# Three more tiles of attention probabilities transposed and split on TensorE, and a smaller slack in the planner

## The chip, the cores and the metric

The kernel runs on one core of one Trainium2 chip. The metric is the device time of one execution in microseconds (us), the median of several runs. Engines carry the names of the profile: PE is TensorE (PEld its weight loads), DVE is VectorE, ACT is ScalarE, POOL is GpSimd, SP is SyncE, which here issues every DMA.

## The reference

Attention within clusters, whose output feeds a feed-forward layer. Queries and keys are each assigned to one of 16 clusters of their head, and a query sees only the keys of its own cluster.

```python
# q, k, v: (4, 8, 768, 64) float32; centroids: (8, 16, 64)
q_assign = argmax(einsum('bhsd,hcd->bhsc', q_n, c_n))      # normalised; the same for k
mask = q_assign[:, :, :, None] == k_assign[:, :, None, :]
scores = where(mask, scale * (q @ k.T), -1e9)
attn = exp(scores - max(scores)); attn = attn / (sum(attn) + 1e-9)
x = (attn @ v).transpose(0, 2, 1, 3).reshape(3072, 512)
h = x @ w_in                                               # (512, 2048)
g = where(h >= 1, h, where(h <= -1, 0, (h + 1) ** 2 / 4))
out = g @ w_out                                            # (2048, 512)
```

## The kernel before

**Units and tiles.** The work is cut into 4 batches, 3 chunks of 256 query rows in each, and 4 pairs of heads: 48 attention units. A unit has 4 score tiles of 128 queries by 768 keys: the two heads `j` of the pair times the two query tiles `t` of the chunk, numbered `n = 2 j + t`. When the 4 head pairs of a chunk are through, their output `x` goes through the feed forward in 8 blocks `f` of 256 hidden columns.

**One score tile.** TensorE makes the scores in a PSUM buffer `pair`, a group of 4 matmuls (`at_scores`); the mask comes in through the second pair of these. VectorE takes them out to `sS` with the row minimum of the negated scores in `sbi`. ScalarE makes the exponential in place and its row sums. The probabilities are then needed transposed and as two halves in float16, a high part and the rest, since the products run in float16 with three terms. There are two ways to that, in `at_soft`:

- By DMA: ScalarE casts `sS` to the high half of `hl`, GpSimd subtracts to the low half, and one transposing DMA brings both to `pT`.
- By TensorE, where `by_tensor` says so: six float32 transposes of `sS` against the identity `idf` go back into the tile's own `pair` buffer, ScalarE casts them to the high half of `pT`, two matmuls with the negated identity `idm` take that half off in place, and a second cast makes the low half. The buffer is held until then.

`at_av` multiplies `pT` with the values into `banka`; ScalarE copies the row factors to `rb`, VectorE multiplies, ScalarE casts the high half of `x`, GpSimd subtracts the low half. `ffn1` makes a hidden block from `x` in one of three banks (`bankh`, `banki`, `bankj`; 24 matmuls), takes it through `r` on VectorE and ScalarE and to `g` in two halves (ScalarE, GpSimd); `ffn2` gathers the products with `w_out` in the second `pair` buffer. So the scores have both `pair` buffers in the prologue (`early()`: steps below 22), and the first one, `pair0`, alone afterwards. The weights are loaded, scaled and split beside all that (`word`, `w`, `wk`, `w_am`, `w_iw`, `w_sw`).

**What sets the order.** Nothing is issued as it is written. Each operation is recorded (all of them at line 322) with a priority, its step. A list planner in the kernel then deals the operations out to the engines: it runs a model with prices, up to 60 rounds of forward and backward passes, and keeps the order that comes out shortest in a replay with noise. `SLACK` is added in the forward pass to the end of every operation that is not a DMA. The order is built into the program; each engine goes through its own in sequence, and waits by semaphores. The first chunk's scores have steps 0 to 15; the second chunk's first head pair has 16 to 19, its second 20 to 23, and a tile's softmax comes one step after its scores.

The lines that the change touches are 39 (`SLACK`) and 960 (the condition of `by_tensor`).

Of the kernel before, what the change touches and what calls it, by code (L numbers as in the profile page):

```python
# [35 lines left out]
PHASES = (0.0, 850.0, 1700.0, 2550.0)  # L36


LATER, LATER_DMA, SLACK = 25, 600, 30


TURN, TURN_WAIT = dict(vector=185, gpsimd=118), 200
# [402 lines left out]
def tile_clustered_attention_moe(  # L445
# [83 lines left out]
    def early():  # L529

        return rec.step < EARLY
# [390 lines left out]
    def at_soft(b, hp, c, j, t):  # L922
# [12 lines left out]
        if by_tensor(b, hp, c, j, t):  # L935
            with rec.group():
                for i in range(T):
                    to = pS[:, i // 3, i % 3 * P : (i % 3 + 1) * P]
                    rec.tensor.matmul(
                        to, sf[:, i * P : (i + 1) * P], idf, start=(i % 3 == 0), stop=False, is_transpose=True,  # L940
                        skip_group_check=True,
                    )
            pt = pS[:, :, :HS].rearrange("p h (n q) -> p h n q", q=P)
            hi, lo = (pT[:, x * T : (x + 1) * T, t, :].rearrange("p (h n) q -> p h n q", h=2) for x in range(2))
            rec.scalar.copy(hi, pt)
            with rec.group():
                for h in range(2):
                    rec.tensor.matmul(pS[:, h, :HS], idm, hi[:, h], start=False, stop=True, skip_group_check=True)
            rec.scalar.copy(lo, pt)
            at_sums(e, n)  # L950
            return
# [5 lines left out]

    def by_tensor(b, hp, c, j, t):

        return early() and b == c == 0  # L960

    def at_sums(e, n):
        if n == 3:
# [317 lines left out]
```

## Time and profile before

| | |
|---|---|
| median of 3 runs | 879.8 us (878.59 to 880.06) |
| the profiled execution, its own time | 879.45 us |
| its span, first to last instruction | 877.7 us |
| TensorE busy | 93% of the span, 7532 matmuls |
| VectorE, ScalarE, GpSimd busy | 75%, 74%, 62% |
| tiles transposed by DMA, by TensorE | 176, 16 |

How to read it: the profile shows one execution. A stretch's busy time tells which engine paces it; what an engine waited for is told by the instruction whose semaphore came last. Matmuls overlap, so the time that a group takes is best read from its start to the start of what follows it. The granted clock is that of TensorE, 1.0 at 2.4 GHz and 0.5 at 1.2 GHz.

### The profile page before, as it was taken

The page shows a single profiled execution, that of the slowest core. Times are in us where ns is not written, and L with a number is a line of the kernel's source. Part 1 is how long each engine was busy: PE and PEld are TensorE (multiplying, and loading weights), DVE is VectorE, ACT ScalarE, POOL GpSimd, SP SyncE. Part 2 cuts the span into 40 slices and gives each one's busy share as a digit, 9 for nine tenths or more (in the row PEclk, how much of TensorE's full clock was granted, in tenths as well). Part 3 has the DMA queues.
Part 4 walks back from the last instruction along what each step waited for, and adds up shares of the span by engine and source line. Part 5 has one row for each costly group of instructions (what it writes and reads, how often), then busy time and mean ns, then how long its engine had stood idle before and what let it go on. Part 6 is the DMA issues. An engine that isn't in the chain of part 4 may idle for free.

```text
span 877.7 us, 19909 instructions
## 1 busy us (share of the span) xinstructions
PE 815.6 (93%) x7532; PEld 565.8 (64%) x7532; DVE 658.1 (75%) x1571; ACT 649.7 (74%) x1150; POOL 540.8 (62%) x534
## 2 busy tenths in 40 slices
PE   3666879899999999999999999999999999999998
PEld 3444556566666766766766666666766667766664
DVE  7999989999779776668787688668887767454232
ACT  6899998788776687777777597788777787676232
POOL 1155497878656778656666676666666667666222
PEclk9999889999999999999999999999999999999999
DMA  9975689779999979899898879999999888676100
GB/s 321 254 198 133 198 176 181 138 148 197 163 182 176 165 142 192 172 174 191 173 204 161 149 129 182 167 173 176 180 182 179 147 150 157 109 133 109 20 25 25
DMA packets 404193, 141.01 MB, mean 161 GB/s; under 512 B 372736, under 2 KB 396288, under 8 KB 404096
## 3 DMA queue, kind: packets, MB, share of 16 engines
q1 hardware_dynamic: 404096, 139.73, 81.2%
q8 instruction: 59, 0.97, 0.4%
q14 instruction: 38, 0.31, 0.1%
HBM read 40.40 MB, written 6.29 MB: 53 GB/s over the span
## 4 chain that ended last, share of the span: by engine, by line
PE 64%; DVE 19%; ACT 6%; DMA 4%; issue 3%; POOL 2%; SPq 0%; ACTq 0%; DVEq 0%; POOLq 0%
PE pair L322 32%; PE banka L322 9%; PE bankh L322 9%; PE bankj L322 7%; PE banki L322 7%; DVE sS L322 5%; DMA pT<-hl 3%; DVE r L322 2%; DVE qn L322 2%; ACT sS L322 2%; POOL hl L322 2%; DVE w L322 1%; DVE banki L322 1%; DVE bankh L322 1%; DVE bankj L322 1%
## 5 line engine op out<-in xcount | busy, mean ns | idle before, releaser
L322 POOL TENSOR_TENSOR hl<-sS,hl 128x768 f16<-128x768 f32 x176 | 295.8, 1687 | 109.8 <-ACT hl L322 83.0
L322 PE MATMUL pair<-w,g 128*128 128x512 f16 x1152 | 270.2, 379 | 0.3 <-ACT o L322 0.3
L322 PEld LDWEIGHTS <-w 128*128 128x128 f16 x2304 | 224.3, 98 | 48.2 <-issue 5.1
L322 ACT ACTIVATE sS<-sS,sbi 128x768 f32<-128x768 f32 x192 | 179.3, 934 | 82.5 <-DVE sbi L322 75.0
L322 DVE CUSTOM_DVE_ANT_0 sS<-pair,zero,er 128x768 f32<-128x768 f32 x192 | 194.1, 1011 | 60.8 <-PE pair L322 46.9
L322 PEld LDWEIGHTS <-g 128*128 128x128 f16 x1152 | 110.4, 98 | 117.2 <-issue 2.1
L322 PE MATMUL pair<-kv,q 128*128 128x384 f16 x768 | 160.4, 333 | 18.5 <-DVE sbi L322 9.0
L322 ACT CAST hl<-sS 128x768 f16<-128x768 f32 x176 | 144.0, 826 | 14.4 <-DMA pT<-hl 12.8
L322 POOL TENSOR_TENSOR g<-r,g 128x512 f16<-128x512 f32 x88 | 102.7, 1167 | 82.8 <-ACT g L322 81.2
L322 PEld LDWEIGHTS <-q 128*128 128x128 f16 x1152 | 84.0, 98 | 76.6 <-issue 31.0
L322 PEld LDWEIGHTS <-kv 128*64 128x64 f16 (+1 forms) x2112 | 104.4, 108 | 6.4 <-issue 2.8
L322 PE MATMUL banka<-pT,kv 128*64 128x256 f16 x1728 | 103.7, 274 | 3.0 <-DMA pT<-hl 3.0
L322 ACT ACTIVATE r<-r,f_ra,f_rs 128x512 f32<-128x512 f32 x88 | 71.2, 810 | 43.2 <-DVE r L322 42.9
L322 ACT CAST g<-r 128x512 f16<-128x512 f32 x88 | 53.7, 610 | 9.2 <-DVE r L322 5.0
L322 PE MATMUL bankj<-x,w 128*128 128x256 f16 x432 | 51.9, 273 | 0.4 <-DVE r L322 0.4
L322 PE MATMUL banki<-x,w 128*128 128x256 f16 x408 | 48.8, 273 | 1.7 <-DVE w_am L322 1.7
L322 POOL TENSOR_TENSOR qn<-qn,phi 128x256 f16<-128x256 f16 x48 | 30.8, 660 | 25.9 <-DVE phi L322 15.3
L322 PE MATMUL bankh<-x,w 128*128 128x256 f16 x312 | 39.7, 281 | 0.0
L322 POOL TENSOR_TENSOR w<-w 128x1024 f16<-128x1024 f32 x12 | 28.0, 2336 | 15.0 <-ACT w L322 15.0
L322 PE MATMUL bankh<-wk,w 128*128 128x256 f16 x312 | 36.8, 273 | 0.0
L322 ACT ACTIVATION_READ_ACCUMULATOR sS<-sS,sbi 128x1 f32 x192 | 36.2, 189 | 0.0
L322 DVE TENSOR_TENSOR rb<-banka,rb 128x256 f32<-128x256 f32 x48 | 20.1, 418 | 20.1 <-ACT rb L322 19.6
(232 smaller groups left out, 1101.9 us busy)
## 6 DMA issues: line engine op xcount, KB each, us to landing
w<-in_moe_w_out_dram SPq DMA_DIRECT2D x14, 512.0 KB, 4.6
q<-in_q_dram SPq DMA_DIRECT2D x12, 512.0 KB, 5.0
kv<-in_k_dram SPq DMA_DIRECT2D x16, 384.0 KB, 4.0
kv<-in_v_dram SPq DMA_DIRECT2D x16, 384.0 KB, 4.3
out_dram<-o SPq DMA_DIRECT2D x11, 512.0 KB, 3.7
w<-in_moe_w_in_dram SPq DMA_DIRECT2D x10, 512.0 KB, 5.7
word<-in_moe_w_in_dram SPq DMA_DIRECT2D x6, 512.0 KB, 5.0
o<-in_v_dram SPq DMA_DIRECT2D x8, 384.0 KB, 4.2
```

The costliest lines, as they stand in the source:

```text
L322: fn(*args, **kw)
```

## The change

```diff
-LATER, LATER_DMA, SLACK = 25, 600, 30
+LATER, LATER_DMA, SLACK = 25, 600, 20
 ...
     def by_tensor(b, hp, c, j, t):
 
-        return early() and b == c == 0
+        return early() and b == 0 and (c == 0 or t == 0)
```

The way by TensorE is opened to the first query tile (`t == 0`) of the first batch's later chunks, as long as the step is below 22. That is true of three tiles: both heads of the second chunk's first head pair (`n` = 0 and 2), and the first head of its second pair (`n` = 0). On ScalarE 3 casts to `hl` go and 6 to `pT` come; on GpSimd 3 subtractions go; on SyncE's queue 3 transposing DMAs go; on TensorE 18 transposes and 6 matmuls with `idm` come. Nothing else is added or removed.

The second edit takes 10 ns off what the planner adds to each operation. Since the planner's list follows from all of its numbers, the order differs on the engines from the early prologue until late in the kernel. Three places follow; a number behind a name is that of its buffer.

GpSimd, around the last `x` of the first chunk (`x0_72`, which the first feed forward needs), before and then now. `hl` are the low halves of second-chunk tiles, `rr` the row factors, `w0` and `word0` weights:

```order
L322 TENSOR_TENSOR rr0_179<-rs3_175,rr0_179 128x4
L322 TENSOR_TENSOR hl0_183<-sS2_87,hl0_183 128x768
L322 TENSOR_TENSOR w0_78<-w0_78 128x1024
L322 TENSOR_TENSOR hl2_185<-sS1_86,hl2_185 128x768
L322 TENSOR_TENSOR hl1_184<-sS0_85,hl1_184 128x768
L322 TENSOR_TENSOR hl0_183<-sS2_87,hl0_183 128x768
L322 TENSOR_TENSOR x0_72<-rb0_182,x0_72 128x256
```

```order
L322 TENSOR_TENSOR rr0_179<-rs3_175,rr0_179 128x4
L322 TENSOR_TENSOR x0_72<-rb0_182,x0_72 128x256
L322 COPY w_all1_223<-w_iw1_2_132 128x2
L322 TENSOR_TENSOR w0_78<-w0_78 128x1024
L322 TENSOR_TENSOR hl0_183<-sS0_85,hl0_183 128x768
L322 TENSOR_TENSOR x0_72<-rb0_182,x0_72 128x256
L322 TENSOR_TENSOR w0_78<-w0_78 128x1024
```

The last `x` stood behind four `hl` and stands behind one (the `x` in the second row is that of the third head pair, which came earlier before).

ScalarE, from the exponential of the second chunk's second head pair, `n` = 0 (`rs1`, `sbi0`), to the end of this tile's way through ScalarE, before and then now:

```order
L322 ACTIVATE sS0_85,rs1_173<-sS0_85,sbi0_168 128x768
L322 ACTIVATE sS1_86,rs1_173<-sS1_86,sbi1_169 128x768
L322 ACTIVATE w0_78<-w0_78,w_sw2_166 128x1024
L322 COPY banki_83<-w_iw0_0_126 128x2
L322 CAST hl2_185<-sS1_86 128x768
L322 CAST w0_78<-w0_78 128x1024
L322 CAST hl1_184<-sS0_85 128x768
```

```order
L322 ACTIVATE sS0_85,rs1_173<-sS0_85,sbi0_168 128x768
L322 ACTIVATE sS1_86,rs1_173<-sS1_86,sbi1_169 128x768
L322 ACTIVATE qn0_67<-q0_65,sq0_142 128x4x64
L322 CAST g0_75<-r0_221 128x512
L322 CAST pT1_177<-pair0_79 128x6x128
L322 COPY banki_83<-w_am0_1_119 128x2
L322 ACTIVATE qn0_67<-q0_65,sq0_142 128x4x64
L322 CAST hl2_185<-sS1_86 128x768
L322 ACTIVATE qn0_67<-q0_65,sq0_142 128x4x64 x2
L322 CAST pT1_177<-pair0_79 128x6x128
```

One cast to `hl` ended the tile's way; now it is two casts out of `pair0`, with eight other instructions between the exponential and the second of them.

ScalarE, around the first feed forward's `r`, before and then now:

```order
L322 ACTIVATE sS2_87,rs1_173<-sS2_87,sbi2_170 128x768
L322 CAST hl0_183<-sS2_87 128x768
L322 ACTIVATE word0_71<-word0_71,w_sw0_164 128x1024
L322 ACTIVATE r0_221<-r0_221,f_ra0_206,f_rs0_211 128x512
L322 ACTIVATE sS0_85,rs1_173<-sS0_85,sbi3_171 128x768
```

```order
L322 ACTIVATE word0_71<-word0_71,w_sw0_164 128x1024
L322 CAST pT0_176<-pair0_79 128x6x128
L322 ACTIVATE r0_221<-r0_221,f_ra0_206,f_rs0_211 128x512
L322 ACTIVATE wk0_69<-w0_78 128x1024
L322 CAST w0_78<-word0_71 128x1024
```

The first `r` stood behind the exponentials of three tiles of the second head pair (`rs1`); it now stands ahead of all of them.

## Rows read from the trace of the kernel before

**Rows 1.** The page: each engine's busy us, share of the span, instructions.
```profile
PE 815.6 (93%) x7532; PEld 565.8 (64%) x7532; DVE 658.1 (75%) x1571; ACT 649.7 (74%) x1150; POOL 540.8 (62%) x534
```
**Rows 2.** By stretch: us, busy of PE, PEld, DVE, ACT, POOL; granted clock, DMA share, GB/s.
```profile
0.00:119.00 119.00, 73.95 (x735) 52.19 (x736) 109.72 (x306) 108.39 (x166) 49.97 (x73) 0.92 0.78 211
119.00:203.00 84.00, 77.16 (x693) 53.76 (x692) 79.18 (x217) 71.02 (x135) 68.85 (x57) 0.98 0.86 167
203.00:878.00 675.00, 664.52 (x6105) 459.88 (x6104) 469.15 (x1051) 470.29 (x854) 421.94 (x405) 1.00 0.82 151
```
**Rows 3.** The same view, shorter stretches of the prologue.
```profile
109.00:116.00 7.00, 3.87 (x48) 2.70 (x43) 6.49 (x14) 7.00 (x13) 6.66 (x4) 1.00 0.37 70
116.00:123.00 7.00, 5.17 (x23) 3.37 (x23) 6.87 (x25) 6.99 (x14) 6.97 (x6) 0.51 1.15 204
123.00:142.00 19.00, 18.85 (x164) 13.20 (x163) 15.89 (x37) 16.79 (x32) 17.93 (x14) 1.00 1.03 231
...
57.60:85.40 27.80, 16.71 (x184) 11.82 (x184) 26.29 (x77) 27.61 (x45) 13.41 (x15) 1.00 0.67 167
```
**Rows 4.** Waits of TensorE, 119 to 240 us: total us, times, longest.
```profile
PE pair L322 <- DVE sbi L322: 4.4, 5, 1.8
```
**Rows 5.** The same view: 240 us to the end, then up to 119 us.
```profile
PE banka L322 <- DMA pT<-hl: 3.0, 2, 2.1
...
PE pair L322 <- ACT pT L322: 14.5, 14, 2.3
```
**Rows 6.** TensorE's timeline around one tile's transposes: start, us, instructions.
```profile
70.10 0.87 PE L322 MATMUL pair<-idf,sS 128*128 128x128 f32 x6 [0.45 <-ACT sS L322]
70.90 0.41 PE L322 MATMUL banka<-idu,rr 128*64 128x128 f16 x8
...
73.21 0.50 PE L322 MATMUL pair<-pT,idm 128*128 128x384 f16 x2
73.55 0.62 PE L322 MATMUL bankh<-wk,ones 128*128 128x128 bf16 x8
```
**Rows 7.** Instructions on `sS` and `pT`: ns least/median/most, first and last start.
```profile
L322 PE MATMUL pair<-idf,sS x96: 272/273/473, 28.7 to 104.0; 128*128 128x128 f32 x96
L322 DVE CUSTOM_DVE_ANT_0 sS<-pair,zero,er x42: 986/1008/1020, 25.5 to 202.0; 128x768 f32<-128x768 f32 x42
L322 ACT ACTIVATE sS<-sS,sbi x41: 917/935/977, 26.9 to 200.8; 128x768 f32<-128x768 f32 x41
L322 ACT CAST hl<-sS x24: 813/828/868, 107.4 to 200.0; 128x768 f16<-128x768 f32 x24
L322 POOL TENSOR_TENSOR hl<-sS,hl x24: 1632/1652/2637, 108.3 to 200.9; 128x768 f16<-128x768 f32 x24
...
L322 ACT CAST pT<-pair x32: 771/790/852, 30.3 to 106.7; 128x768 f16<-128x768 f32 x32
```
**Rows 8.** TensorE's timeline into the first feed forward (`bankh<-x,w`).
```profile
117.83 1.44 PE L322 MATMUL pair<-kv,q 128*128 128x384 f16 x4 [1.95 <-DVE sbi L322]
119.06 4.70 PE L322 MATMUL bankh<-x,w 128*128 128x256 f16 x24
123.60 0.81 PE L322 MATMUL pair<-kv,q 128*128 128x384 f16 x4
124.25 2.78 PE L322 MATMUL bankj<-x,w 128*128 128x256 f16 x24
```
**Rows 9.** Timelines of ScalarE and GpSimd around the last `x` before it.
```profile
116.56 0.43 ACT L322 CAST x<-rb 128x256 f16<-128x256 f32 x1
...
112.99 5.33 POOL L322 TENSOR_TENSOR hl<-sS,hl 128x768 f16<-128x768 f32 x3
118.28 0.67 POOL L322 TENSOR_TENSOR x<-rb,x 128x256 f16<-128x256 f32 x1
```
**Rows 10.** TensorE's timeline, the two longest waits between 119 and 203 us.
```profile
143.67 0.81 PE L322 MATMUL pair<-kv,q 128*128 128x384 f16 x4 [1.79 <-DVE sbi L322]
...
157.62 1.47 PE L322 MATMUL banki<-x,w 128*128 128x256 f16 x12 [1.67 <-DVE w_am L322]
```

## The prediction

> **What bounds the kernel now.** I read the views in this order: the page's busy times, the busy time by stretch with the granted clock, the waits of TensorE, and then the timelines around the first feed forward. TensorE is busy for 815.6 us [rows 1] of a span of 877.7. By stretch there are three regimes [rows 2]. From 203 us to the end TensorE is busy for 664.5 of 675 us, so there every microsecond of matmul that is added or taken away moves the end. Up to 119 us, where the first feed forward starts, TensorE works for 74.0 of 119 us, while VectorE is busy for 109.7 and ScalarE for 108.4: those two pace the prologue. Between 119 and 203 us it is mixed: TensorE 77.2 of 84, VectorE 79.2 of 84. TensorE's idle time is the second thing to see: 45 us ahead of 119 us, 6.8 us from there to 203 us, 10.5 us in all the rest [rows 2]. From 119 to 240 us 4.4 us of it wait for VectorE's row minimum, which empties the one score buffer [rows 4]. So the end is the start of the first feed forward, plus the TensorE work that is then left, plus the idle time and the half clock that follow.
>
> **Sum made against what.** The profiled execution took 879.45 us for a span of 877.7, so 1.75 us lie around it; the median of the runs is 879.8, 0.35 above. I work in differences and add them to 879.8.
>
> **Part 1, three tiles go to TensorE.** The flag that limits the new path is the step of the score, so of the second chunk's units only three tiles qualify: two of the first head pair and one of the second. The built program bears that out: 114 transposes of `sS` for 96, 38 multiplications with `idm` for 32, and 173 for 176 of the `hl` casts, subtractions and transposing DMAs.
> TensorE: the six transposes of a tile take 0.80 us from their start to the start of what follows, the two `idm` matmuls 0.34 us [rows 6], so 1.14 us a tile and 3.4 us for three at the full clock. At half clock a single transpose takes 473 ns where its median is 273 [rows 7], and the other end is 2 x 3.4 = 6.9 us. I take 3.4, since the half-clock stretches are short [rows 3].
> ScalarE: two casts `pT` of 790 ns take the place of one `hl` of 828 ns [rows 7], 0.75 us a tile, 2.3 us in all. Two of the tiles fall where ScalarE has no idle time (7.00 of 7.00 us busy from 109 to 116 us [rows 3]).
> GpSimd: three subtractions of 1.65 us go [rows 7], 4.9 us. DMA: three transposing transfers go. After 240 us, TensorE's waits for such transfers sum to 3.0 us in 2 [rows 5]; up to 240 us that view has none, so fewer of them there are worth nothing.
>
> **Part 2, the order is dealt anew.** The slack goes from 30 to 20 ns in the planner. By itself that is nothing, but the list that it writes differs on the engines from about 22 us to about 765 us. I counted what stands ahead of the first feed-forward matmul. On TensorE there stood 23 score groups and 16 transposed tiles; now 21 and 18, the last without its `idm`. A score group takes 0.65 us to the next start [rows 8], so 2 x 0.65 go and 2 x 0.80 + 0.34 come: 0.6 us more is done by then, and of the 3.4 us some 2.8 us are left behind it.
> When does that first matmul start? In the trace at 119.06 us [rows 8], and what it needs last is the low half of `x`: ScalarE's cast is done at 116.99 us, but GpSimd comes to it at 118.28 us, behind a run of `hl` subtractions [rows 9]. In the new order one subtraction stands there, not four, so these 1.3 us go. Against that, VectorE's multiply ahead of the cast now comes as its 305th instruction, not its 292nd: the feed forward's small scales and a weight operation were brought forward, one reduction was put back, 1.8 us more in sum, with each kind at its mean in the trace. Net +0.5 us; bounds -1.3 us (VectorE's share hidden) to +2.3 us (GpSimd's gain not had, ScalarE's 0.5 us of extra work ahead of that cast on top).
> What follows it: the first `r` on ScalarE stands 3 exponentials and 5 `hl` casts earlier, with 4 `pT` casts more ahead of it, so the feed forward's products and their evacuation move ahead of the scores. From the 22nd to the 32nd score group TensorE has 5 to 14 us more work in front of each than before; by about the 42nd group, at 203 us, both orders have done nearly the same. That backlog is what could fill waits. Of the 6.8 us I let go the longest wait for the score buffer, 1.8 us, and the one for `w_am`, 1.7 us [rows 10]; both lie in the middle of that backlog. The others lie where the orders are about to meet again, and stay. So 3.5 us go; bounds: none, or all 6.8.
> After 203 us the deal is new too, with no reason for either sign; I take the 10.5 us as they are, and 2 us either way.
>
> **The sum.** +0.5 (start) + 2.8 (work behind it) - 3.5 (waits filled) = -0.2 us; 879.8 - 0.2 = 879.6, rounded to **879.5 us**.
>
> **The clock.** The granted clock fell to half (0.51 over 116 to 123 us [rows 3]) after 7 us in which TensorE worked for 3.87 us, and the first 24 feed-forward matmuls ran in 4.70 us where the next 24 took 2.78 [rows 8]; with the score group ahead of them (1.44 us for 0.81) that stretch cost 2.5 us. I leave it as it is. Over 57.6 to 85.4 us the clock was 1.00 with TensorE busy for 16.7 of 27.8 us, some of it transposes [rows 3].
> The Trainium skill has a rule that speaks against this change ("TensorE: Matmul & The Clock Gate", Part 4: PE-mode transpose): a transpose there takes 275 to 390 ns and does not count as activity for the clock gate. The first half does not hold here, where six take 0.80 us; the second the trace neither shows nor refutes, since other matmuls stand among the transposes.
>
> **The rivals.**
> Faster: the backlog hides more. If 6.0 of the 6.8 us go, the sum is 0.5 + 2.8 - 6.0 = -2.7, 877.1 us; if the added work also keeps the clock up from 116 to 123 us, another 2.5 us go, 874.6 us. For it: counted the same way, VectorE has 1 us less to do up to the 42nd score, and GpSimd loses 5 us where it was busy for 6.66 of 7.00 us [rows 3]. Against it: VectorE was itself busy for 79.2 of 84 us, so there is little to fill from.
> Slower, by the score buffer: a tile on TensorE keeps its PSUM buffer `pair0` until its second cast. Row by row that is score 0.81, minimum 1.01, exponential 0.94, transposes 0.87, cast 0.79, `idm` 0.50, cast 0.79 = 5.7 us, against 1.8 us where the minimum frees it [rows 6 to 8]. For the third tile ScalarE's new order puts eight other instructions between exponential and second cast; at 0.4 to 0.9 us each (an estimate from the neighbours in rows 7 and 9) and partly under the matmuls that makes nearly 9 us. What covers it on TensorE between that score and the next is 36 feed-forward matmuls, an output group and the tile's own, about 8 us. It decides from where the chain is longer than that cover; then the excess, up to the 4 us that a tile holds the buffer longer, is idle time: 879.5 + 4.0 = 883.5 us. For it: there is no margin, and in the prologue, with two buffers, TensorE waited 14.5 us in 14 waits for such casts [rows 5]. Against it: there it had no feed forward to put between.
> Slower, by the clock: the added transposes do not hold it, the start slips, and half clock lies over 7 us of feed forward more than now: 2.5 us as above, 879.5 + 2.5 = 882.0 us. For it: the work ahead of 116 us stays thin. Against it: from 123 to 142 us TensorE is busy for 18.85 of 19 us at full clock [rows 3].
> That the change doesn't do what it says is excluded by the counts above.
>
> **How the numbers follow.** Forecast, near 879.5: 0.40. Faster rival, 874.6 to 877.9: 0.35. Buffer rival: 0.17. Clock rival: 0.08. A difference of 0.2%, 1.8 us, is about what a measurement of this kernel can tell from no change, so faster 0.35, same 0.40, slower 0.25. The range leaves out a tenth at either end: from 875.0 (most of the faster rival) to 884.0 (the buffer rival whole).
>
> **What would show it.** In the profile after: the last `idm` matmuls at about 130 us; the first feed-forward matmul between 118 and 121 us; TensorE's idle time from there to 203 us at 3 to 4 us; the `x` subtraction right behind its cast; full clock after 123 us. I am wrong if the first feed forward starts later than 121 us, if the waits for the row minimum after 119 us grow beyond 4.4 us, or if waits for transposing DMAs grow by several us, which would be the new deal and not the tiles.

## The result, and the profile after

The changed kernel takes 882.7 us, median of 8 runs (880.8 to 883.4), beside 879.9 us of the kernel before on the same chip. The ratio is 1.0026, interval 1.0015 to 1.0037: slower by a quarter of a percent, where the forecast was a shade faster (-0.2 us in its sum). The time lies inside the predicted range and 3.2 us above the predicted 879.5. The profiled execution took 883.11 us for a span of 881.2, against 879.45 and 877.7 before, so the two traces differ by 3.5 us of span.

Busy time of each engine on the page of the changed kernel, to set beside [rows 1]:

```profile
PE 819.0 (93%) x7556; PEld 568.1 (64%) x7556; DVE 655.1 (74%) x1571; ACT 652.3 (74%) x1153; POOL 534.3 (61%) x531
```

TensorE is busy 3.3 us longer (818.96 against 815.63 us, summed over the stretches below), ScalarE 2.6 us longer and GpSimd 6.5 us less. The prediction had counted +3.4, +2.3 and -4.9. Now the stretches of the changed kernel, cut at its first feed-forward matmul; columns as in [rows 2]:

```profile
0.00:121.82 121.82, 75.01 (x742) 53.16 (x743) 110.37 (x308) 107.64 (x162) 47.76 (x71) 0.90 0.71 202
121.82:203.00 81.18, 73.93 (x682) 51.70 (x680) 75.52 (x205) 69.89 (x131) 62.87 (x54) 1.00 0.76 154
203.00:881.20 678.20, 670.02 (x6137) 463.21 (x6135) 469.22 (x1060) 474.79 (x862) 423.69 (x408) 1.00 0.80 151
```

The same cut of the kernel before, at its own first feed-forward matmul and at its span's end:

```profile
0.00:119.06 119.06, 74.01 (x736) 52.19 (x736) 109.78 (x306) 108.45 (x166) 50.03 (x73) 0.92 0.78 211
119.06:203.00 83.94, 77.09 (x693) 53.76 (x692) 79.12 (x217) 70.96 (x134) 68.79 (x57) 0.98 0.86 167
203.00:877.70 674.70, 664.52 (x6105) 459.88 (x6104) 469.15 (x1051) 470.29 (x854) 421.94 (x405) 1.00 0.82 151
```

From these six rows the 3.5 us add up. The first feed forward starts 2.76 us later. TensorE is busy behind it for 73.93 + 670.02 = 743.95 us against 741.61: +2.34. Its idle time from that start to 203 us is 81.18 - 73.93 = 7.25 us against 6.85: +0.40. From 203 us on it is 8.18 us against 10.18: -2.00. Sum: +3.50.

The idle time as a whole is therefore the same, 62.24 us against 62.08, and what is left over is the 3.3 us of busy time. But two changes cancel in it. Cut at 240 us, TensorE idles for 56.95 us up to there against 52.28 before (+4.67), and from there on for 5.29 us against 9.80 (-4.51). By itself this sum would also fit a loss that is simply the tiles' own work; the experiments have to tell.

The waits of TensorE between 119 and 240 us in the changed kernel, where [rows 4] had 4.4 us for the row minimum (`sbi`); columns: total us, times, longest:

```profile
PE pair L322 <- DVE sbi L322: 5.3, 8, 2.0
PE pair L322 <- ACT o L322: 1.4, 1, 1.4
PE banki L322 <- DVE wk L322: 1.3, 1, 1.3
PE pair L322 <- ACT sS L322: 1.2, 1, 1.2
```

The same view from 240 us to the end. The 3.0 us of waits for transposing DMAs [rows 5] are gone:

```profile
PE banki L322 <- ACT n L322: 0.3, 1, 0.3
PE bankj L322 <- DVE has L322: 0.2, 1, 0.2
```

And the two waits of the changed kernel that lead from 0 to 240 us, where the kernel before has 14.5 us in 14 waits for `pT` [rows 5] and, in the row printed apart, 3.9 us for `sS`:

```profile
PE pair L322 <- ACT pT L322: 15.1, 15, 2.1
PE pair L322 <- ACT sS L322: 14.2, 11, 2.5
```

```profile
PE pair L322 <- ACT sS L322: 3.9, 5, 1.1
```

So in the changed kernel TensorE's transposes wait 10 us more for ScalarE's exponentials. Only 2.4 us of that stand at the three tiles (1.22 and 1.21 us, below), so more than 7 us of it are other tiles'. The thirteenth score group on TensorE's timeline, before and after:

```profile
83.07 0.81 PE L322 MATMUL pair<-kv,q 128*128 128x384 f16 x4 [0.96 <-ACT pT L322]
```

```profile
88.64 0.95 PE L322 MATMUL pair<-kv,q 128*128 128x384 f16 x4 [2.05 <-ACT pT L322]
```

It starts 5.6 us later; 1.6 us of that is work that now stands ahead of it (TensorE is busy for 50.74 us up to there, against 49.19). The first of the three tiles has its transposes only at 111.46 us:

```profile
111.46 0.88 PE L322 MATMUL pair<-idf,sS 128*128 128x128 f32 x6 [1.22 <-ACT sS L322]
...
121.11 0.87 PE L322 MATMUL pair<-idf,sS 128*128 128x128 f32 x6 [1.21 <-ACT sS L322]
121.82 2.78 PE L322 MATMUL bankh<-x,w 128*128 128x256 f16 x24
...
130.48 0.82 PE L322 MATMUL pair<-idf,sS 128*128 128x128 f32 x6
...
133.54 0.50 PE L322 MATMUL pair<-pT,idm 128*128 128x384 f16 x2
```

The question for the experiments is then: is it the three tiles that cost the time, or the order that the planner writes anew when anything in its input changes?

### The profile page after: what moved, and what is told of

The parts are those of the page before. It is cut to its first block, busy times and chain, and to the rows that moved or that the text cites. A ratio compares the mean times of both kernels' runs of the same rounds, so it can differ in the third digit from the quotient of the medians.

```text
span 881.2 us, 19955 instructions
## 1 busy us (share of the span) xinstructions
PE 819.0 (93%) x7556; PEld 568.1 (64%) x7556; DVE 655.1 (74%) x1571; ACT 652.3 (74%) x1153; POOL 534.3 (61%) x531
## 4 chain that ended last, share of the span: by engine, by line
PE 74%; DVE 14%; ACT 7%; issue 3%; DMA 1%; POOL 1%; ACTq 0%; SPq 0%; DVEq 0%; POOLq 0%
PE pair L322 37%; PE banka L322 11%; PE bankh L322 9%; PE banki L322 9%; PE bankj L322 9%; DVE sS L322 3%; ACT sS L322 2%; ACT w L322 1%; DVE r L322 1%; DVE qn L322 1%; DVE wk L322 1%; ACT pT L322 1%; DVE w L322 1%; DVE bankh L322 1%; ACT wk L322 1%
## 5 line engine op out<-in xcount | busy, mean ns | idle before, releaser
L322 POOL TENSOR_TENSOR hl<-sS,hl 128x768 f16<-128x768 f32 x173 | 287.4, 1666 | 113.0 <-ACT hl L322 90.5
L322 POOL TENSOR_TENSOR g<-r,g 128x512 f16<-128x512 f32 x88 | 105.1, 1194 | 74.2 <-ACT g L322 74.0
L322 ACT CAST hl<-sS 128x768 f16<-128x768 f32 x173 | 141.7, 825 | 4.0 <-DMA pT<-hl 2.6
L322 PE MATMUL bankh<-x,w 128*128 128x256 f16 x312 | 37.7, 273 | 0.9 <-DVE r L322 0.9
L322 POOL TENSOR_TENSOR w<-w 128x1024 f16<-128x1024 f32 x12 | 27.3, 2272 | 14.5 <-ACT w L322 14.5
L322 DVE TENSOR_SCALAR r<-bankh,f_lo,f_hi 128x512 f32<-128x512 f32 x30 | 24.2, 808 | 15.2 <-PE bankh L322 9.4
```

The lines of the kernel that those rows point to most:

```text
L322: fn(*args, **kw)
```

## Experiments

**The theories.** Deal (theory O in the expectations): any new order of the prologue (all work up to about 240 us) loses some microseconds against the one that stood there, tiles or not; the tiles' own work is absorbed. Work (theory W): the added TensorE and ScalarE work, or the tiles' hold on the score buffer `pair0`, makes the loss. The score group that the expectations call the twelfth is the thirteenth in this count. In each set of runs the kernel before stood beside on the same chip, at 880.6 to 881.1 us.

### Each half of the change alone

`old20` has the new slack and no tile on the new path; `new30` has the tiles and the old slack.

```diff
 (old20, against before)
-LATER, LATER_DMA, SLACK = 25, 600, 30
+LATER, LATER_DMA, SLACK = 25, 600, 20
 (new30, against after)
-LATER, LATER_DMA, SLACK = 25, 600, 20
+LATER, LATER_DMA, SLACK = 25, 600, 30
```

> The kernel before with the slack at 20 ns alone: no tile moves, only the order is dealt anew, on its own. Theory W: the work is that of before, so 879 to 881 us, TensorE busy 815.6 us. Theory O: a deal moves the time by some us by itself; it need not be this deal's sign, so anything from 876 to 884 us, with the prologue's twelfth score group off 83.1 us by several us.

> The three tiles on TensorE with the slack left at 30 ns, dealt on its own. Theory W: 882 to 883.5 us, TensorE busy 819 us, since the work is the same whatever the order. Theory O: what this deal gives, 878 to 884 us; a time below 880.5 us would speak against W.

`old20` took 882.6 us (ratio 1.0020, 1.0008 to 1.0033), `new30` 883.5 us (1.0034, 1.0021 to 1.0047). Each half alone costs about what both cost together. The halves don't add, so neither is a fixed price. The slack alone, with not one operation of arithmetic changed, brings most of the loss. `new30` by itself does not separate the theories: its time, 883.5 us, fits the ranges of both. The sign expected in `old20` did not come: its thirteenth score group starts at 84.28 us, 1.2 us off 83.07, and in `new30` the twelfth and thirteenth run together from 82.52 us. So the late thirteenth group is the changed order's own and no common sign of the loss.

### The slack at two other values

The kernel before with `SLACK` 25 and 35, to see whether `old20` was one bad draw:

> The kernel before with the slack at 25 ns alone: one more deal of the old work. Theory O (deals differ by some us and the one of before is a good one among them): 881 to 884 us. Theory W: same work, 880 to 881 us.

> The kernel before with the slack at 35 ns alone: a third new deal of the old work. Theory O: 881 to 884 us, and not the same as at 20 or 25 ns. Theory W: 880 to 881 us.

884.7 us (1.0037, 1.0021 to 1.0054) and 885.3 us (1.0044, 1.0026 to 1.0061), both a little above the 881 to 884 us expected by the deal theory and far from the 880 to 881 of Work. Four values of the slack for the same arithmetic spread over half a percent, with no trend: 882.6 us for 20, 884.7 for 25, 880.6 to 881.1 for 30 (before) and 885.3 for 35. That of before is the lowest of the four. The granted clock does not explain it: its mean over all runs was 0.982 in `old20` and 0.983 in `old25`, beside 0.983 in the kernel before on the same chips. In `old35` it was lower, 0.976, so part of that loss may be the clock. No run tells how 30 was chosen; if it was by trying, the order of before is a picked draw, and a new one is likely to be worse.

### Added work without a new order

`pe_early` keeps every row of before's order and computes five score groups of the prologue twice, some 3.2 us of TensorE; `act_early` writes the `hl` cast of three tiles twice, some 2.5 us of ScalarE.

```diff
 (pe_early, behind each score group)
+        if b == 0 and c == 1 and (hp == 0 or (hp == 1 and n == 0)):
+            rec.nodes[-1].calls *= 2
 (act_early, behind the cast)
+        if b == 0 and c == 1 and (hp == 0 and t == 0 or hp == 1 and n == 0):
+            rec.nodes[-1].calls *= 2
```

> The kernel before in its own order, with the score groups of five tiles of the second chunk (its first head pair and the first tile of the second) made twice into the same buffer: 3.25 us more TensorE work ahead of the first feed forward, no other engine touched. Theory W: most of it shows, 882.5 to 883.5 us. Theory O: it goes into TensorE's idle time there (4 us of waits between 111 and 118 us), 879.9 to 880.9 us.

> The kernel before in its own order, with ScalarE's cast to hl made twice for the same three tiles of the second chunk: 2.5 us more ScalarE work, as much as the changed tiles bring, nothing else touched. If ScalarE's extra work is what delays the first feed forward: 2 to 2.5 us more, ratio 1.0025. If it is absorbed: ratio 0.999 to 1.001. Theory O says absorbed.

880.5 us (0.9996, 0.9985 to 1.0006) and 880.6 us (0.9995, 0.9985 to 1.0005). Neither can be told from before. As much work as the tiles add on TensorE and on ScalarE does not move the end, each by itself and where no buffer is held for longer. It was not hidden ahead of the first feed forward, though, as `pe_early`'s expectation had it. In its profiled execution that starts 4.0 us later than before:

```profile
123.08 4.09 PE L322 MATMUL bankh<-x,w 128*128 128x256 f16 x24
```

Of these 4.0 us 2.3 were there at the thirteenth score group (85.4 us), ahead of all doubled matmuls. Yet the span, 878.9 us, is only 1.2 us longer. Behind that start TensorE was busy 0.9 us less and, after 240 us, idle 2.1 us less (7.71 us against 9.80). So a late first feed forward need not make a late end.

`after_no_pe` goes the other way: the changed kernel's order, with the 18 transposes and 6 halving matmuls of the three tiles left out (their probabilities are not computed); the copies out of `pair0` stay, as scaled copies of the same size (median 795 ns, the casts 799).

```diff
+            if c:
+                n1, n2, n3, n4 = rec.nodes[-4:]
+                n1.calls, n3.calls = [], []
...
```

> The changed kernel in its own order, with the transposes and the idm matmuls of the three tiles left out (24 matmuls, 3.4 us); ScalarE's two casts per tile stay, at the same place and on the same buffer, so these tiles' probabilities are wrong and nothing else differs. Theory W (the added TensorE work shows in the end): 3 us below the changed kernel, 0.9992 to 1.0 of the kernel before. Theory O (the order): the work is absorbed as it was when score groups were doubled, so the changed kernel's ratio stays, 1.0015 to 1.003.

885.3 us (1.0054, 1.0037 to 1.0070). Taking TensorE's work away gives nothing back; the run is even 2.5 us above the changed kernel, and outside the ranges of both theories. It does not acquit the tiles' work, because the clock was not equal: its mean over the runs was 0.979, against 0.982 in the changed kernel. In the profiled executions (first `after_no_pe`, then the changed kernel) it was 0.84 and 0.90 up to 119 us, and with 3.2 us of matmuls left out TensorE was busy for 818.4 us all the same. In that execution what was taken away came back as slower matmuls.

```profile
0.00:119.00 119.00, 72.93 (x699) 52.59 (x701) 107.50 (x297) 103.27 (x154) 42.20 (x69) 0.84 0.73 204
0.00:119.00 119.00, 73.49 (x731) 52.17 (x732) 107.58 (x303) 104.83 (x158) 45.43 (x69) 0.90 0.71 204
```

### The order and the tiles exchanged

`after_dma` keeps the changed kernel's order and puts the three tiles back on cast, subtraction and transposing DMA. `tiles_in_before` is the reverse: every step stands where it stood before, and only the three tiles are on TensorE. `tib_nope` is that kernel without the tiles' transposes and halving matmuls, with their copies kept.

```diff
 (tiles_in_before, against after: the planner's search gives way to a fixed place for each step)
-        best = None
-        for _ in range(ROUNDS):
...
+        ready, self.order = [(KEY[x.i], x.i) for x in self.nodes if not x.preds], []
...
```

> The changed kernel's order, dealt as there (slack 20, three tiles planned for TensorE), but the three tiles go by ScalarE's hl cast, GpSimd's subtraction and the transposing DMA as before: 3.4 us of TensorE work and 2.3 us of ScalarE work are taken out again and every other instruction stands where it stood. Theory W (the added TensorE work itself, not hidden, is what the end moved by): 3 us less than the changed kernel, 879 to 880 us. Theory O (the new order of the prologue is what lost it, the twelfth score group being 5.5 us later before any of the three tiles begins): 882 to 883 us, as the changed kernel. TensorE's idle time tells which: about 57.7 us under W, about 61 us under O.

> The changed kernel's arithmetic in the order of the kernel before: every step stands where it stood before, and only the three tiles' six-transpose groups and two halving matmuls each stand on TensorE where the cast, the subtraction and the transposing DMA stood. Score groups that need the score buffer pair0 move behind the tile that holds it (four of them, by one to three places); everything else keeps its row. Theory that the new deal of the order costs the time and the tiles' work does not: within 0.2% of before, 879 to 882.3 us. Rival, that the three tiles' work or their hold on pair0 costs the time: slower by 0.25 to 0.5%, 882.7 to 885 us, with TensorE's waits for VectorE's row minimum between 119 and 240 us grown by 2 us or more.

> tiles_in_before without TensorE's 18 transposes and 6 halving matmuls of the three tiles: the two copies of each tile out of pair0 are kept, so that ScalarE's work and the hold on the score buffer stay. (The three tiles' probabilities are left out by this.) If the 9.4 us of tiles_in_before are the hold on pair0 and the score groups that stand behind it: at least 6 us of them stay, 886.5 to 891 us. If they are TensorE's work, directly or through a half-clock stretch that it brings on: they go, 880 to 884 us.

`after_dma` took 895.1 us (1.0164, 1.0146 to 1.0183), `tiles_in_before` 890.4 us (1.0111, 1.0092 to 1.0130), `tib_nope` 888.9 us (1.0102, 1.0083 to 1.0121). For `tiles_in_before` the deal theory had expected no change, and it failed: the tiles in an order that wasn't made for them cost 9.4 us, more than its rival's 882.7 to 885 us as well. For `after_dma` both theories missed by 12 us or more. In `tib_nope` 8.2 us stay without any TensorE work of the tiles, as expected of the hold. What stays then is ScalarE's copies and `pair0`, held until the second copy, with the score groups that had to move behind it. TensorE's waits from 100 to 140 us show part of it, for `tiles_in_before`, then `tib_nope`, then the kernel before (total us, times, longest):

```profile
PE pair L322 <- ACT pT L322: 6.5, 5, 2.1
PE pair L322 <- ACT sS L322: 3.0, 1, 3.0
PE pair L322 <- DVE sbi L322: 1.3, 1, 1.3
```

```profile
PE pair L322 <- ACT pT L322: 6.8, 5, 3.0
PE bankj L322 <- DVE wk L322: 4.0, 1, 4.0
PE pair L322 <- DVE sbi L322: 2.4, 2, 1.3
PE banka L322 <- POOL rr L322: 1.1, 1, 1.1
```

```profile
PE pair L322 <- DVE sbi L322: 3.2, 2, 1.9
PE pair L322 <- ACT pT L322: 2.0, 3, 0.9
PE bankj L322 <- DVE wk L322: 1.8, 1, 1.8
```

The waits for the copies (`pT`) grow from 2.0 to 6.5 and 6.8 us; the longest wait of `tib_nope`, for `wk`, is not of that kind. In `tiles_in_before` the granted clock adds to it: from 100 to 142 us it was 0.75 and TensorE busy for 30.01 us; before it was 0.88 and 35.16. Over the whole span `tiles_in_before` is busy 8.4 us longer than before (3.2 of it the tiles' own matmuls) and idle 2.5 us longer, `tib_nope` 3.5 and 6.3. So the loss shows mostly as slower matmuls in the one and mostly as waits in the other, and how much of it the hold alone makes is open. First `tiles_in_before`, then before:

```profile
100.00:142.00 42.00, 30.01 (x224) 20.93 (x222) 26.41 (x62) 31.19 (x50) 18.25 (x15) 0.75 0.48 135
```

```profile
100.00:142.00 42.00, 35.16 (x279) 23.68 (x279) 36.90 (x94) 39.54 (x70) 35.52 (x27) 0.88 0.92 217
```

`after_dma` is the reverse: the tiles' old path in an order that was not made for it. Its waits from 100 to 240 us lead with the row minimum (9.0 us against 5.3 in the changed kernel over the same stretch), and GpSimd, which gets its subtractions back, is waited for too:

```profile
PE pair L322 <- DVE sbi L322: 9.0, 7, 3.8
PE pair L322 <- ACT pT L322: 5.3, 4, 2.1
PE banka L322 <- POOL rr L322: 3.7, 1, 3.7
PE bankh L322 <- POOL x L322: 2.8, 1, 2.8
```

Here too a part is the clock: TensorE is busy for 821.9 us, 2.9 us longer than in the changed kernel, with 3.2 us of matmuls less; up to 119 us it was granted 0.86, against 0.90.

Order and path belong together: exchange one alone and 9.4 or 14.5 us are lost; let the planner deal anew for the tiles and all but 3 us come back.

### Where the loss sits: prologue and later part of two orders joined

The order is one list, so two lists can be joined: one up to the first score group of the second batch (232.7 us before, 243.4 after), the other for all that is left. `sp_b_a` is before's prologue with the changed kernel's later part, `sp_a_b` the reverse, `sp_b_n30` before's prologue with the later part of `new30`. `sp_o20_a` and `sp_n30_a` put the prologues of `old20` and `new30` ahead of the changed kernel's later part. The arithmetic is that of the kernel whose prologue it is (before's in `sp_b_a`, `sp_b_n30` and `sp_o20_a`).

```diff
-        best = None
-        for _ in range(ROUNDS):
...
+        self.order = [self.nodes[i] for i in ORDER]
```

> The arithmetic of the kernel before throughout; its own order up to the first score group of the second batch (232.7 us before), from there the order of the changed kernel. Deal theory: the prologue of before and the later part of after add up, TensorE's idle time comes to about 52.3 + 0.8 = 53 us of which 4.6 us less than before, 875.5 to 878 us, ratio 0.994 to 0.997. Rival, that the idle time after 240 us in the kernel before is the return of what its prologue saved (the data arrive when they arrive): no gain, 879.5 to 882 us, idle time again about 57 us.

> The same splice with the later part taken from the order that has the three tiles on TensorE and the old slack (its idle time behind that point was 0.4 us). Deal theory: 875.5 to 878 us. Rival, idle time only handed on: 879.5 to 882 us.

> The changed kernel's arithmetic; its own order up to the first score group of the second batch, from there the order of the kernel before. Deal theory: the worse prologue with the worse later part, idle time 56.9 plus up to 5.4 us, 884 to 888 us. Rival, idle time only handed on: as the changed kernel, 882 to 884 us.

> The arithmetic of the kernel before; the prologue of the order with slack 20 alone (no tile moved), then the changed kernel's later part, the same that stands in sp_b_a. If the slack's new deal makes the prologue's loss: 881 to 884 us, near the changed kernel's 882.7. If it is the three tiles: near sp_b_a, 876 to 878.5 us.

> The changed kernel's arithmetic; the prologue of the order with the three tiles and the old slack 30, then the changed kernel's later part. If any new deal of the prologue loses about 5 us, tiles or not: 881 to 884.5 us. If the tiles cost nothing and only slack 20 deals badly: near sp_b_a, 876 to 879 us.

| prologue | later part of before | later part of after |
|---|---|---|
| of before | 881.0 us (1) | 876.6 us, 0.9955 (0.9937 to 0.9972) |
| of `old20` (no tile moved) | not run | 884.1 us, 1.0039 (1.0019 to 1.0059) |
| of `new30` (tiles moved) | not run | 883.7 us, 1.0041 (1.0026 to 1.0055) |
| of after (tiles moved) | 885.9 us, 1.0068 (1.0043 to 1.0092) | 882.7 us, 1.0026 (1.0015 to 1.0037) |

`sp_b_n30` took 878.5 us (0.9972, 0.9961 to 0.9984), half a microsecond above the range expected. The cells come from different chips, so the ratios are compared, each against the kernel before on its own chip. Read down, the changed kernel's prologue costs 0.68% (6.0 us) in front of one later part and 0.71% (6.3 us) in front of the other. Read across, its later part gains 0.45% and 0.42% (4.0 and 3.7 us). So the loss sits in the prologue, and some two thirds of it are given back later by an order that no longer touches the tiles. In front of one and the same later part the three new prologues lie within 0.15% (1.3 us) of each other, one of them without any tile on the new path, and 0.71 to 0.86% above that of before. That is the deal theory: what the loss shares is the new prologue, not the tiles. `sp_o20_a` scattered from 878.6 to 887.8 us, so its place within the three is loose. What the tiles add to a prologue is not shown within the microsecond or two that these intervals leave.

The later part is seen in the traces. TensorE from 240 us to the end in `sp_b_a`, whole list, where before waits 3.0 us for transposing DMAs [rows 5]:

```profile
PE pair L322 <- DVE sbi L322: 1.2, 1, 1.2
PE bankh L322 <- DMA q<-qn: 0.7, 1, 0.7
PE banki L322 <- ACT n L322: 0.4, 1, 0.4
PE bankj L322 <- DVE has L322: 0.2, 1, 0.2
```

The waits for transposing DMAs are gone here too, with all 176 transposing transfers in place. So three transfers fewer are not needed for that; the later order does it. (Even in before's own order they were 1.1 us in `pe_early`.) `sp_b_a` beats both kernels, with the arithmetic of before and nothing moved to TensorE.

## Why the prediction was off, point by point

**The work and its price: right.** Read from start to next start, the tiles' six groups take 3.2 us in the changed kernel (0.71 and 0.33, 0.71 and 0.32, 0.75 and 0.34), for 3.4 predicted. The busy time rose by 3.3 us, 2.3 of it behind the first feed forward, for 2.8 predicted; busy time alone would not prove it, since in the profile of `old20` it rose by 3.7 us with no tile moved, at a lower clock. `pe_early` and `act_early` show that such amounts need not move the end.

**The start of the first feed forward: the step that failed first.** The prediction set +0.5 us, with bounds to +2.3. Measured: +2.76 us, at 121.82 us, which crosses the 121 us named there as a sign of being wrong. Of that 1.00 us is more work ahead of it (0.6 predicted) and 1.76 us is more idle time. Other executions of the same two prologues bear the sign out, not the size: 118.86 and 120.39 us in `sp_b_a` and `sp_b_n30`, 121.55 us in `sp_a_b`. The step counted instructions ahead of `x` on VectorE and GpSimd at their mean durations, as if a new order had no new waits. GpSimd's part came as described, with its subtraction right behind the cast:

```profile
120.96 0.39 ACT L322 CAST x<-rb 128x256 f16<-128x256 f32 x1
```

```profile
121.43 1.13 POOL L322 TENSOR_TENSOR x<-rb,x 128x256 f16<-128x256 f32 x1 [0.49 <-ACT x L322]
```

But the cast itself starts 4.4 us later than in [rows 9], and TensorE comes to the feed forward straight from the second tile's transposes, which had waited 1.21 us for their exponential. The lateness was there at the thirteenth score group, before any tile: it starts at 83.1 to 85.4 us in the order of before (`before`, `act_early`, `pe_early`) and at 88.6 to 91.9 us in the changed one (`after`, `after_dma`, `after_no_pe`). The order on all engines had changed from 22 us on, and the prediction looked at it only near the feed forward. Its premise, that the end follows this start, does not hold as it stands either: in `pe_early` the start was 4.0 us later and the end 1.2 us.

**The waits filled: the step that failed most.** -3.5 us predicted, +0.4 measured: TensorE idles for 7.25 us from the first feed forward to 203 us, where 3 to 4 us were named as the sign of being right. The backlog itself did come: in front of the 22nd to the 32nd score group TensorE had done 4 to 15 us more work than before, for 5 to 14 predicted. The idle time did not shrink by it. The two waits of [rows 10] did go in their places, and others came: up to 240 us 5.3 us in 8 for the row minimum instead of 4.4 in 5, which was the second sign of being wrong, and waits for `o`, `wk` and `sS` that before did not lead. That a backlog takes away the longest waits was a guess; here it moved them.

**After 203 us: at its bound.** Taken as unchanged, 2 us either way; measured -2.0 us: +2.5 up to 240 us, most of it one wait of 2.0 us for the row minimum at 207.28 us, and -4.5 behind. It is a result of the deal too, as the joined orders show. No term of the prediction stands for it, so that the time still fell inside the range is in part luck.

**The clock: near.** The prediction left the half clock over 116 to 123 us [rows 3] as it was. It went; the granted clock there is now 1.00. A later stretch took its place: after 4 us in which TensorE worked for 1.99, it fell to 0.51 for 3.4 us at full load. Three rows of the changed kernel:

```profile
116.00:123.00 7.00, 5.48 (x47) 3.66 (x44) 6.74 (x15) 7.00 (x13) 5.64 (x3) 1.00 0.37 122
205.00:209.00 4.00, 1.99 (x13) 0.93 (x11) 3.72 (x7) 4.00 (x9) 3.17 (x4) 0.96 0.25 54
208.60:212.00 3.40, 3.40 (x10) 1.20 (x9) 1.69 (x6) 3.01 (x7) 1.40 (x2) 0.51 0.91 173
```

So the 2.5 us of one place became some 1.7 us (half of 3.4) at the other. The rule of the Trainium skill ("TensorE: Matmul & The Clock Gate", Part 4) stays as open as it was: no run here isolates transposes from the matmuls around them. The prediction's remark that its first half does not hold compared two different things: one transpose takes 273 ns here [rows 7], near the low end of the 275 to 390 ns that the prediction cites; what is shorter is the step from one to the next, with six in 0.80 us.

**The rivals.** The time, 882.7 us, lies next to two of them, 883.5 and 882.0. The nearness is no proof of either. The buffer rival's mechanism can cost that much: in the fixed order of `tib_nope` 8 us go with the hold and the copies, slower matmuls included. But in the changed kernel it isn't what shows: the third tile's transposes run at 130.48 us without a wait, and up to 142 us no wait of TensorE behind the first feed forward is longer than 0.5 us. The clock rival wanted more half clock over the feed forward; there was less. The faster rival asked for the backlog to hide 6.0 us; it hid none.

**What stays open.** Shown is that a new order of the prologue loses time with no tile moved. How it loses is not: why before's prologue beats the others was not traced to one instruction, and slower matmuls and waits share the loss differently in each execution. The waits for ScalarE's exponentials grow in the changed kernel (3.9 to 14.2 us up to 240 us), but no run moved these alone. What share of the changed kernel's own 2.8 us is the tiles' work is open, and so is whether the tiles would pay in a prologue dealt as well as that of before: `tiles_in_before` is no such order, and none was found.

## What to carry to other kernels

When a change makes a planner deal the whole order anew, its effect is the change plus a draw: run the planner's constant alone, and the change with the old constant, before giving the time to the operations. Compare the two traces where the orders first differ, not where the changed operations stand. And where one order is good early and another late, join them at a point that both reach: here that gave 876.6 us, better than either, with no change of arithmetic.

## What the runs showed of the hardware

In the first 50 us `before`, `tiles_in_before`, `tib_nope` and `sp_b_a` issue the same instructions, yet the granted clock of that stretch was 0.93, 0.86, 0.97 and 0.93 in the four profiled runs. The second and the last ran on the same chip. Their rows, in that order:

```profile
0.00:50.00 50.00, 27.95 (x272) 20.17 (x273) 44.53 (x136) 40.44 (x62) 9.94 (x37) 0.93 0.94 280
```

```profile
0.00:50.00 50.00, 27.26 (x268) 19.69 (x269) 44.13 (x135) 40.06 (x61) 9.95 (x37) 0.86 0.92 274
```

```profile
0.00:50.00 50.00, 27.85 (x272) 19.92 (x273) 44.47 (x136) 40.40 (x62) 10.00 (x37) 0.97 0.92 279
```

```profile
0.00:50.00 50.00, 28.02 (x272) 20.15 (x273) 44.86 (x136) 40.66 (x62) 9.96 (x37) 0.93 0.93 280
```

Here, where TensorE is busy for some 28 of 50 us, the half clock differs from run to run, and a part of the scatter of equal runs goes with it: the 12 of `sp_o20_a` spread over 9 us, the fastest at a mean granted clock of 0.989, the three slowest at 0.972 to 0.977. The 8 of the changed kernel spread over 2.5 us, at 0.980 to 0.984. One profiled run can't settle a difference of a few microseconds in such a stretch.
